# Loading sorted tokens in blocks of 128 slots, with a last block rounded up to sixteens, in place of equal blocks

## The chip, the cores and the metric

The kernel runs on one core of a Trainium2 chip. The core has a matrix engine (PE, whose weight loads are listed apart as PEld), a vector engine (DVE), a scalar engine (ACT), a general engine (POOL) and a queue engine that issues most transfers (SP). Transfers are carried by 16 DMA engines that all queues share. The metric is the device time of one execution in microseconds (us), given as the median of several runs.

## The reference

Three layers run one after the other on 4 sequences of 768 tokens: a gated linear attention, a mixture of eight experts in which each token goes to one expert, and a last layer whose product is normalised.

```
def _moe_ref(x, expert_emb, tau, w1, w2):              # x: 3072 x 384
    xn = x / (np.linalg.norm(x, axis=-1, keepdims=True) + 1e-06)
    en = expert_emb / (np.linalg.norm(expert_emb, axis=-1, keepdims=True) + 1e-06)
    logits = xn @ en.T / tau
    expert_idx = np.argmax(logits, axis=1)
    ...
    for e in range(E):                                  # 8 experts
        mask = expert_idx == e
        h = np.maximum(x[mask] @ w1[e], 0.0)            # 384 -> 1024
        out[mask] = gate_w[mask, None] * (h @ w2[e])    # 1024 -> 384

def reference(**kwargs):
    attn_out = _attn_ref(**attn_kwargs)                 # state = f * state + k v ; y = q state
    x = attn_out.transpose(0, 2, 1, 3).reshape(B * S, H * D)
    x = _moe_ref(x=x, **moe_kwargs)
    return _moe2_ref(x=x, **moe2_kwargs)                # x @ w_in, softmax times x, layer norm, @ w_out
```

## The kernel before

**Attention (lines 109 to 365).** Pairs of heads and chunks of 128 tokens are worked through in steps. At the end of a chunk the tokens' rows of 384 features (1.5 KB) stand in SBUF, and `route` gives each token a slot of its expert. An indirect transfer (L413) scatters the rows into `xs` in memory. Slot r of expert e is row 8r + e of `xs`, so the rows of one expert lie eight rows apart.

**Turns.** The experts are worked through in eight turns, ordered by falling numbers of tokens. The numbers of slots that a turn handles are fixed: `CAPS = (460, 432, 412, 404, 396, 392, 384, 378)`. I number the turns from 0, so turn 2 has 412 slots and turn 3 has 404. A turn has eight chunks of 128 hidden features. For each chunk g, `w_load` fetches a piece of the two weights (`w1s`, `w2s`, 192 KB each, two buffers each), `w_split` splits them into a high and a low part (ACT `w1h` L544, POOL `w1l` L545, ACT `w2h` L546, DVE `w2l` L547), `l1` makes nine products into `h` (L773), ACT and DVE make `hh` and `hl` from it (L777, L778), and `l2` adds nine products to `yacc` (L792), one chunk behind `l1`.

**The sorted tokens.** `x_load(e)` fetches a turn's rows of `xs` into `xin`, in equal blocks of slots: `NBLK` is 4 blocks for turns of more than 384 slots and 3 for the others. That makes 108 rows in a block for turn 1, 103 for turn 2, 101, 99, 98, then 128 for turn 6 and 126 for turn 7. One transfer brings all blocks of a turn; its partition dimension is the number of rows in a block. `x_T(e, kc)` transposes the blocks on PE into `xps` (L758), for each of the three pieces kc of 128 features, from where ACT and DVE split them into the turn's `xT` tiles (`x0h`/`x0l` for even turns, `x1h`/`x1l` for odd ones, L759, L760). `x_load(e + 2)` and the last `x_T(e + 1)` are emitted in the fifth chunk of turn e.

**Turn 0** goes another way: `x0_load` fetches its 460 slots in four transfers of 115 rows each (L475), before the last tokens are routed; `x0_in` adds them by products with the identity to `x0T` in PSUM (L488), and `x0_sel` adds the tokens of the last two chunks by products with indicators (L483).

**Order.** A scheduler that simulates the program in time fixes each engine's order of instructions when the kernel is built; on the chip each engine runs its list in order and stops at the first instruction whose inputs are not there. SP's list holds the loads of weights, tokens and of the next layer's weights (`d`, L855, decoded in between by DVE and POOL), so a transfer is issued only when everything ahead of it on SP has been issued.

```
def rows(buf, t):
    r = buf.rearrange("(r e) d -> e r d", e=E)[which(t), 0:CAPS[t], :]
    return r.rearrange("o (i p) d -> p (o i) d", i=NBLK[t])
```

Of the kernel before, what the change touches and what calls it, by code (L numbers as in the profile page):

```python
# [8 lines left out]
F32 = mybir.dt.float32  # L9
# [7 lines left out]
PSUM = bass.MemoryType.PSUM  # L17
DRAM = bass.MemoryType.DRAM

B, H, S, D = 4, 8, 768, 48  # L20
NP = H // 2            # head pairs
D2 = 2 * D             # features of a pair
DP = 64 + D            # their partitions: a head's features at 0, the other's at 64
GROUPS = (((0, 1), (1, 2), (2, 4)), ((0, 2), (2, 4)), ((0, 4),), ((0, 4),))   # head pairs of each batch, in turn
LEAD = 3
R = 6                  # consecutive tokens on a partition of the transposed loads
NPART = S // R         # 128
R2 = R // 2
CH = 128               # chunk of the linear attention
NCH = S // CH          # 6  # L30
E = 8
DM = H * D             # 384
F = 1024
NT = B * S             # 3072
CAP = 464              # slots of an expert on the fast path
# slots of the experts in the order of their turns: first the one that is ahead after FIRST tiles
# of tokens, then the others by falling numbers of tokens
CAPS = (460, 432, 412, 404, 396, 392, 384, 378)
FIRST = (B - 1) * NCH + 1
CT = 4  # L40
CTP = CAPS[0] // CT    # 115
NBLK = tuple(CT if n > 384 else 3 for n in CAPS)    # blocks of a turn's slots
NSLOT = E * CAP
KC = DM // 128         # 3
FC = F // 128          # 8
NTILE = B * NCH        # 24

# [35 lines left out]
def _build(ctx, tc, ins, outs):  # L83
    nc = tc.nc
    PE, DVE, ACT, POOL, SP = nc.tensor, nc.vector, nc.scalar, nc.gpsimd, nc.sync
# [13 lines left out]
    meta = dram.tile([NT, 2], F32, name="meta")     # a sorted token's number and gate  # L99
# [7 lines left out]
    ident = cst["ident"]  # L107

    # ------------------------------------------------------------------ attention
# [10 lines left out]
    loaded = {}  # L120
# [8 lines left out]
    # the pairs' features beside each other, with nothing between the heads' but zeros  # L129
# [9 lines left out]
    # persistent little tiles  # L139
# [21 lines left out]
    # the steps before the end at which the experts' first weights are loaded and split  # L161
# [3 lines left out]
    # stage A: per (batch, head pair), decays and scaled transposed q and k  # L165
# [70 lines left out]
    def stage_units():  # L236
        """the work that prepares the pairs, in the order of its emission"""
        last = B * NP
        u = [lambda: a_R(0), lambda: a_F(0), lambda: (a_G(0), a_K(0), a_Q(0), a_R(1))]
        for n in range(last):  # L240
            def hs0(n=n):
                if n + 1 < last:
                    a_F(n + 1)
            def hs1(n=n):
                if n > 0:
                    a_K(n)
                if n + 1 < last:
                    a_G(n + 1)
            def hs2(n=n):
                if n > 0:  # L250
                    a_Q(n)
                if n + 2 < last:
                    a_R(n + 2)
            u += [hs0, hs1, hs2]
        return u

    # stage B: steps (batch, head pairs, chunk)
# [113 lines left out]
    def route(b, c0, c1):  # L371
        """the chunks' tokens to slots of their experts: a list of small pieces of work"""
# [49 lines left out]
        # the gate  # L422
# [26 lines left out]
    def first():  # L449
        """the expert of the first turn: the one with the most tokens by now"""  # L450
        pc = psT.tile([128, E], F32, tag="t", name="counts0")
        PE.matmul(pc, lhsT=onesb, rhs=cum, start=True, stop=True)
        key, mx, num = (rp.tile([128, n], F32, tag="f" + t, name="f_" + t) for t, n in (("key", E), ("mx", 1), ("num", 1)))
        perm = rp.tile([1, 1], I32, tag="fperm", name="f_perm")
        DVE.scalar_tensor_tensor(key, pc, float(E), cst["small"][:, 0:E], ALU.mult, ALU.add)
        DVE.tensor_reduce(out=mx, in_=key, axis=AX.X, op=ALU.max)
        DVE.tensor_scalar(lead, key, mx[:, 0:1], None, ALU.is_equal)
        DVE.tensor_tensor(key, lead, cst["small"][:, E:], ALU.mult)
        DVE.tensor_reduce(out=num, in_=key, axis=AX.X, op=ALU.add)
        DVE.tensor_copy(perm, num[0:1])  # L460
        turn.extend(nc.values_load_multi_w_load_instructions(
            perm, engines=(mybir.EngineType.SP,), min_val=0, max_val=E - 1)[1])
        DVE.tensor_scalar(cst["row0"], cst["row0"], num[:, 0:1], None, ALU.add)

    # the first turn's tokens: those of the last chunks go to their columns by products with
    # their places' indicators, the others come from memory, and all meet in PSUM
    x0 = {}
    NEAR = 1               # of its blocks, those that go ahead of the last chunk's routing
    rank_after = [None]

    def x0_load():
        src = rows(xs, 0)
        x0["in"] = [tmp.tile([CTP, 2, DM], F32, tag="P", name=f"x0_{i}") for i in range(2)]
        for i in range(CT):
            SP.dma_start(x0["in"][i // 2][:, i % 2, :], src[:, i, :])  # L475
        x0["ps"] = [psA.tile([128, CAP], F32, tag="A", name=f"x0T_{kc}")[:, 0:CAPS[0]] for kc in range(KC - 1)]
        x0["ps"].append(psB.tile([128, CAP], F32, tag="kt", name="x0T_2")[:, 0:CAPS[0]])
        x0["n"] = 0
# [6 lines left out]
    def x0_in():  # L485
        def rows_in(i):
            for kc in range(KC):
                PE.matmul(x0["ps"][kc][:, i * CTP:(i + 1) * CTP], lhsT=x0["in"][i // 2][:, i % 2, kc * 128:kc * 128 + 128],  # L488
                          rhs=ident[:CTP, :CTP], start=False, stop=False)
        for kc in range(KC):  # L490
            x0_sel(NCH - 2, kc, False)
        for i in range(NEAR):
            rows_in(i)
        with tc.issue_after(rank_after[0]):
            for i in range(NEAR, CT):
                rows_in(i)
# [17 lines left out]
    # ------------------------------------------------------------------ experts' weights  # L514
# [4 lines left out]
    def which(t):  # L519
        """the expert of a turn"""  # L520
        return bass.ds(turn[t], 1)

    def rows(buf, t):
        """a turn's slots in memory"""
        r = buf.rearrange("(r e) d -> e r d", e=E)[which(t), 0:CAPS[t], :]
        return r.rearrange("o (i p) d -> p (o i) d", i=NBLK[t])

# [24 lines left out]
    # ---- program: prologue  # L552
# [41 lines left out]
    # normalised expert embeddings over tau into the projection matrix  # L594
# [18 lines left out]
    # how far the preparation of the pairs has to be at a step's end  # L613
# [67 lines left out]
    # ------------------------------------------------------------------ experts  # L681
    w2p = ctx.enter_context(tc.tile_pool(reuse_waits="tile", name="w2p", bufs=1, side="right"))
    xt2p = ctx.enter_context(tc.tile_pool(reuse_waits="tile", name="xt2", bufs=3, side="right"))
    # the experts' products, features by sorted tokens; what a turn writes past its own tokens the
    # next one covers
# [17 lines left out]
    def order():  # L703
        """the experts by falling numbers of tokens, after the first turn's"""
# [24 lines left out]
        # the sorted place of an expert's first token, by expert and by turn  # L729
# [13 lines left out]
    def x_load(e):  # L743
        n = NBLK[e]
        xin[e] = xinp.tile([128, CT, DM], F32, tag="xin", name=f"xin_{e}")[0:CAPS[e] // n, 0:n]
        SP.dma_start(xin[e], rows(xs, e))

    def x_T(e, kc):
        n, nb = CAPS[e], NBLK[e]
        bt = n // nb  # L750
        if kc == 0:
            xT[e] = xT[0] if e % 2 == 0 else xT1
        hi, lo = xT[e]
        if kc == 0:
            xps[e] = psX.tile([128, 2, 512], F32, tag="X", name=f"xps_{e}")
        ps = xps[e][:, kc % 2, 0:n]
        for i in range(nb):
            PE.transpose(ps[:, i * bt:(i + 1) * bt], xin[e][:, i, kc * 128:(kc + 1) * 128], ident[:bt, :bt])  # L758
        ACT.copy(hi[:, kc, 0:n], ps)  # L759
        DVE.tensor_tensor(lo[:, kc, 0:n], ps, hi[:, kc, 0:n].bitcast(F32), ALU.subtract)  # L760
# [22 lines left out]
    def l2(g):  # L783
        """the second product, features by slots"""
# [13 lines left out]
    # the sorted tokens' numbers and gates  # L798
    def rank_tokens():
        """the tokens' sorted places"""  # L800
# [34 lines left out]
    # second layer's weights: float64 words to float32, split in two parts  # L835
# [7 lines left out]
    def decode(u):  # L843
        """one part of a weight, in four steps that are emitted apart"""
# [32 lines left out]
    # every other tile's products stay in the one place, the others' in the other  # L877
# [18 lines left out]
    def m_sm(t, g):  # L896
        """g: the rows' gate, which scales all of a row's products alike"""
# [75 lines left out]
    # ------------------------------------------------------------------ last layer  # L973
# [197 lines left out]
    # is the fast path's answer good for these inputs?  # L1171
# [80 lines left out]
```

## Time and profile before

| | |
|---|---|
| three runs | 796.67, 800.58, 803.06 us, median 800.58 us |
| span of the profiled execution, first to last instruction | 776.1 us |
| time of the profiled execution outside its span | not listed for this execution; the median less the span is 24.5 us |
| PE busy | 676.3 us (87%) |
| DVE, ACT, POOL busy | 485.1, 377.0, 187.2 us |
| attention and routing | about the first 235 us of the span |
| the eight turns of the experts | about 235 to 535 us |
| last layer | the rest |

The span is what the trace covers. A line of waits says which engine stood still, for whom, how long in total, how often, and the longest. A row of the timeline gives the start, the duration, the engine and line, the operation, and in brackets the idle time just before it with what ended it. [...]

### The profile page before, as it was taken

To read this page: it belongs to the slowest core of one execution; us is meant where nothing else is said; L and a number is where in the kernel's file an instruction comes from. 1 tells how busy PE (TensorE), PEld (TensorE's weight loads), DVE (VectorE), ACT (ScalarE), POOL (GpSimd) and SP (SyncE) were. 2 spreads that over 40 slices of the span, in tenths; PEclk is the share of its full clock that TensorE was granted. 3 is DMA by queue.
4 is the path that set the end of the run, shared out by engine and by line. 5 is a ranking of instruction groups with operands and counts; after the bars stand their busy time and mean duration, and the time that the engine had idled before them with its cause. 6 is when DMAs were issued, how large, how long until landed. Compare 5 with 4: busy or idle time off the path is not lost.

```text
span 776.1 us, 12508 instructions
## 1 busy us (share of the span) xinstructions
PE 676.3 (87%) x4336; PEld 600.9 (77%) x4336; DVE 485.1 (63%) x1136; ACT 377.0 (49%) x913; POOL 187.2 (24%) x214
## 2 busy tenths in 40 slices
PE   4999999999887808509797999999999999999995
PEld 3766778778776608509697998999889999999994
DVE  3578778876757208507676776867576555666662
ACT  4668877764532205204343554553554445545452
POOL 4001031030516104406465333332011111111111
PEclk9999999999978768859997999999999999999998
DMA  9964436231432314214656565441000000000000
GB/s 193 359 199 126 122 113 160 62 93 21 144 93 80 105 61 122 71 51 109 140 106 148 127 176 158 141 138 52 0 22 21 21 22 21 21 30 23 21 22 35
DMA packets 91614, 72.29 MB, mean 93 GB/s; under 512 B 34788, under 2 KB 87334, under 8 KB 91542
## 3 DMA queue, kind: packets, MB, share of 16 engines
q1 hardware_dynamic: 87701, 61.94, 29.8%
q0 software_dynamic: 3840, 9.47, 3.4%
q8 instruction: 36, 0.59, 0.3%
q14 instruction: 37, 0.30, 0.2%
HBM read 56.23 MB, written 15.16 MB: 92 GB/s over the span
## 4 chain that ended last, share of the span: by engine, by line
issue 31%; PE 28%; DMA 19%; DVE 11%; ACT 4%; POOL 4%; SPq 1%; POOLq 0%; ACTq 0%; DVEq 0%
DMA w1s<-in_moe_w 15%; PE yacc L792 5%; PE h L773 5%; PE A L276 4%; POOL out L1020 3%; PE y L326 3%; PE px L349 2%; DVE w2l L547 2%; DVE G L211 2%; PE y L322 2%; DMA xin<-xs 2%; PE tf L173 1%; PE u L299 1%; PE tq L173 1%; DMA x<-xs 1%
## 5 line engine op out<-in xcount | busy, mean ns | idle before, releaser
L545 POOL TENSOR_TENSOR w1l<-w1s,w1h 128x384 fp32r<-128x384 f32 x64 | 67.1, 1049 | 168.1 <-ACT w1h L544 159.3
L547 DVE TENSOR_TENSOR w2l<-w2s,w2h 128x384 fp32r<-128x384 f32 x64 | 50.1, 783 | 70.3 <-ACT w2h L546 66.7
L544 ACT CAST w1h<-w1s 128x384 fp32r<-128x384 f32 x64 | 32.8, 513 | 118.9 <-DMA w1s<-in_moe_w 118.7
L792 PE MATMUL yacc<-hh,w2h 128*128 128x460 f32 (+7 forms) x192 | 72.6, 378 | 20.0 <-ACT hh L777 20.0
L1020 POOL DMA_INDIRECT out<-ot,rows x24 | 23.3, 973 | 211.0 <-ACT ot L1018 169.0
L792 PE MATMUL yacc<-hh,w2l 128*128 128x460 f32 (+7 forms) x192 | 70.4, 367 | 0.0
L1015 PE MATMUL o<-wout_h,lh 128*128 128x384 f32 x192 | 64.9, 338 | 0.3
L1015 PE MATMUL o<-wout_h,ll 128*128 128x384 f32 x192 | 64.9, 338 | 0.1
L1015 PE MATMUL o<-wout_l,lh 128*128 128x384 f32 x192 | 64.7, 337 | 0.0
L792 PE MATMUL yacc<-hl,w2h 128*128 128x460 f32 (+7 forms) x192 | 55.6, 365 | 6.9 <-DVE hl L778 6.9
L778 DVE SCALAR_TENSOR_TENSOR hl<-h,hh 128x460 fp32r<-128x460 f32 (+7 forms) x64 | 36.7, 574 | 38.3 <-ACT hh L777 38.1
L891 PE MATMUL h<-win_h,x2h 128*128 128x512 f32 x144 | 58.8, 408 | 0.7 <-DVE rr L905 0.7
L1006 DVE TENSOR_TENSOR ll<-lT,lh 128x512 fp32r<-128x512 f32 x48 | 31.2, 686 | 44.4 <-ACT lh L1005 44.4
L891 PE MATMUL h<-win_h,x2l 128*128 128x512 f32 x144 | 56.9, 395 | 0.0
L891 PE MATMUL h<-win_l,x2h 128*128 128x512 f32 x144 | 56.7, 394 | 0.0
L792 PEld LDWEIGHTS yacc<-hh,w2h 128*128 128x128 f32 x192 | 38.7, 202 | 21.4 <-ACT hh L777 20.3
L276 PE MATMUL A<-Q,K 48*128 48x128 f32 x384 | 52.2, 316 | 0.0
L777 ACT ACTIVATE hh<-h 128x460 fp32r<-128x460 f32 (+7 forms) x64 | 32.8, 512 | 37.0 <-PE h L773 26.2
L758 PE MATMUL xps<-c_ident,xin 108*128 108x108 f32 (+6 forms) x78 | 13.0, 287 | 40.9 <-DMA xin<-xs 39.9
L278 DVE TENSOR_TENSOR Am<-A,c_cmask 128x256 f32<-128x256 f32 (+2 forms) x84 | 35.8, 456 | 17.7 <-PE A L276 11.3
L276 PEld LDWEIGHTS A<-Q,K 48*128 48x128 f32 x384 | 38.0, 199 | 10.7 <-issue 5.1
L792 PEld LDWEIGHTS yacc<-hl,w2h 128*128 128x128 f32 x192 | 37.9, 201 | 9.0 <-DVE hl L778 8.0
(238 smaller groups left out, 1809.1 us busy)
## 6 DMA issues: line engine op xcount, KB each, us to landing
w1s<-in_moe_w SPq DMA_DIRECT2D x64, 192.0 KB, 3.5
w2s<-in_moe_w SPq DMA_DIRECT2D x64, 192.0 KB, 3.0
xs<-zt SPq DMA_DIRECT2D x14, 384.0 KB, 5.5
ldf<-in_f_logit SPq DMA_DIRECT2D x16, 288.0 KB, 3.1
ldk<-in_k SPq DMA_DIRECT2D x16, 288.0 KB, 3.4
ldq<-in_q SPq DMA_DIRECT2D x16, 288.0 KB, 4.4
v<-in_v SPq DMA_DIRECT2D x24, 192.0 KB, 2.7
d<-in_moe_w_in SPq DMA_DIRECT2D x6, 512.0 KB, 4.2
```

Source lines behind the costliest of these rows:

```text
L276: PE.matmul(pa[h][:, j], lhsT=Kc[j][rows_], rhs=Qc[rows_, j], start=True, stop=True)
L278: DVE.tensor_tensor(Am[:, h], pa[h], cst["cmask"].rearrange("p (o c) -> p o c", o=1).to_broadcast([CH, nj, CH]), ALU.mult)
L544: ACT.copy(ah, a)
L545: split_after[0] = POOL.tensor_tensor(al, a, ah.bitcast(F32), ALU.subtract).ins
L547: DVE.tensor_tensor(bl, b, bh.bitcast(F32), ALU.subtract)
L773: PE.matmul(ps, lhsT=wt[:, kc, :], rhs=xx[:, kc, 0:nt], start=(n == 0), stop=(n == 3 * KC - 1))
L777: ACT.activation(hh, ps, AF.Relu)
L778: dec_after[0] = DVE.scalar_tensor_tensor(hl, ps, 0.0, hh.bitcast(F32), ALU.max, ALU.subtract).ins
L792: PE.matmul(yacc[dc], lhsT=wt[:, dc * 128:(dc + 1) * 128], rhs=a, start=(fc == 0 and p == 0), stop=(fc == FC - 1 and p == 2))
L891: PE.matmul(hps[t][:, sl], lhsT=xx[:, kc, :], rhs=wt[:, kc, sl], start=(n == 0), stop=(n == 3 * KC - 1))
L1015: PE.matmul(ps, lhsT=a[:, fc, :], rhs=wt[:, fc, :], start=(n == 0), stop=(n == 3 * FC - 1))
L1020: ins_ = POOL.indirect_dma_start(out=out, out_offset=bass.IndirectOffsetOnAxis(ap=rows2[:, t, 0:1].bitcast(I32), axis=0), in_=ot, in_offse ...
```

## The change

Blocks of a turn's slots are now of 128 rows, and the last block holds what is left over: 76 slots in turn 0, 48, 28, 20, 12 and 8 in turns 1 to 5, a full block in turn 6 and 122 in turn 7. The new `rows_load` fetches all blocks of more than 112 slots by one transfer on 128 partitions. A smaller last block has a transfer of its own, with its number of rows rounded up to a multiple of 16 (80 rows in turn 0; 48, 32, 32, 16, 16 in turns 1 to 5). The transposes and the products with the identity take the same blocks, without the rounding. Turns 6 and 7 have no second transfer.

```
-CTP = CAPS[0] // CT    # 115
-NBLK = tuple(CT if n > 384 else 3 for n in CAPS)    # blocks of a turn's slots
...
     def x0_load():
-        src = rows(xs, 0)
-        x0["in"] = [tmp.tile([CTP, 2, DM], F32, tag="P", name=f"x0_{i}") for i in range(2)]
+        x0["in"] = [tmp.tile([128, 2, DM], F32, tag="P", name=f"x0_{i}") for i in range(2)]
         for i in range(CT):
-            SP.dma_start(x0["in"][i // 2][:, i % 2, :], src[:, i, :])
+            rows_load(x0["in"][i // 2][:, i % 2:i % 2 + 1, :], 0, i, i + 1)
...
         def rows_in(i):
+            bt = block(0, i)
             for kc in range(KC):
-                PE.matmul(x0["ps"][kc][:, i * CTP:(i + 1) * CTP], lhsT=x0["in"][i // 2][:, i % 2, kc * 128:kc * 128 + 128],
-                          rhs=ident[:CTP, :CTP], start=False, stop=False)
+                PE.matmul(x0["ps"][kc][:, i * 128:i * 128 + bt], lhsT=x0["in"][i // 2][:bt, i % 2, kc * 128:kc * 128 + 128],
+                          rhs=ident[:bt, :bt], start=False, stop=False)
...
-    def rows(buf, t):
-        """a turn's slots in memory"""
-        r = buf.rearrange("(r e) d -> e r d", e=E)[which(t), 0:CAPS[t], :]
-        return r.rearrange("o (i p) d -> p (o i) d", i=NBLK[t])
+    def block(t, i):
+        return min(128, CAPS[t] - i * 128)
+
+    def rows_load(dst, t, i0, i1):
+        src = xs.rearrange("(r e) d -> e r d", e=E)
+        full = [i for i in range(i0, i1) if block(t, i) > 112]
+        if full:
+            n = len(full)
+            r = src[which(t), i0 * 128:(i0 + n) * 128, :]
+            SP.dma_start(dst[:, 0:n, :], r.rearrange("o (i p) d -> p (o i) d", p=128))
+        for i in range(i0 + len(full), i1):
+            bt = -(-block(t, i) // 16) * 16
+            r = src[which(t), i * 128:i * 128 + bt, :]
+            SP.dma_start(dst[0:bt, i - i0, :], r.rearrange("o p d -> p (o d)"))
...
     def x_load(e):
-        n = NBLK[e]
-        xin[e] = xinp.tile([128, CT, DM], F32, tag="xin", name=f"xin_{e}")[0:CAPS[e] // n, 0:n]
-        SP.dma_start(xin[e], rows(xs, e))
+        xin[e] = xinp.tile([128, CT, DM], F32, tag="xin", name=f"xin_{e}")
+        rows_load(xin[e], e, 0, -(-CAPS[e] // 128))
...
-        for i in range(nb):
-            PE.transpose(ps[:, i * bt:(i + 1) * bt], xin[e][:, i, kc * 128:(kc + 1) * 128], ident[:bt, :bt])
+        for i in range(-(-n // 128)):
+            bt = block(e, i)
+            PE.transpose(ps[:, i * 128:i * 128 + bt], xin[e][:bt, i, kc * 128:(kc + 1) * 128], ident[:bt, :bt])
```

On SP, around the load of turn 2's tokens in turn 0, this stands before (an ISA row computes the address of the transfer behind it):

```order
L533 ISA
L533 DMA w2s_3541<-in_moe_w 128x384
L746 ISA
L746 DMA xin_3549<-xs 103x4x384
L531 ISA
L531 DMA w1s_3584<-in_moe_w 128x3x128
```

and this now:

```order
L544 ISA
L544 DMA w2s_3542<-in_moe_w 128x384
L533 ISA
L533 DMA xin_3550<-xs 128x3x384
L537 ISA
L537 DMA xin_3550<-xs 32x384
L542 ISA
L542 DMA w1s_3586<-in_moe_w 128x3x128
```

The load has become two, at the same place, and the next weights come behind both.

On SP, around the load of turn 3's tokens in turn 1, before (`d_3` is a part of the last layer's weights):

```order
L531 DMA w1s_3901<-in_moe_w 128x3x128
L855 DMA d_3_4118<-in_moe_w_in 128x512
L533 ISA
L533 DMA w2s_3903<-in_moe_w 128x384
L746 ISA
L746 DMA xin_3911<-xs 101x4x384
```

and now:

```order
L542 DMA w1s_3857<-in_moe_w 128x3x128
L865 DMA d_3_4121<-in_moe_w_in 128x512
L544 ISA
L544 DMA w2s_3859<-in_moe_w 128x384
L542 ISA
L542 DMA w1s_3903<-in_moe_w 128x3x128
L544 ISA
L544 DMA w2s_3905<-in_moe_w 128x384
L533 ISA
L533 DMA xin_3913<-xs 128x3x384
L537 ISA
L537 DMA xin_3913<-xs 32x384
```

Here `d_3` has moved ahead by one chunk's pair of weight loads as well.

On PE, where turn 3's first piece is transposed within turn 1, before:

```order
L773 MATMUL h_3953<-x1h,w1l_3892 128x432
L773 MATMUL h_3953<-x1l,w1h_3891 128x432
L758 MATMUL xps_4174<-c_ident,xin_3911 128x101 x4
L792 MATMUL yacc_0_3775<-hh_3923,w2h_3846 128x432
L792 MATMUL yacc_0_3775<-hh_3923,w2l_3847 128x432
L792 MATMUL yacc_1_3779<-hh_3923,w2h_3846 128x432
```

and now:

```order
L783 MATMUL h_3956<-x1h,w1l_3894 128x432
L783 MATMUL h_3956<-x1l,w1h_3893 128x432
L768 MATMUL xps_4177<-c_ident,xin_3913 128x128 x3
L768 MATMUL xps_4177<-c_ident,xin_3913 128x20
L802 MATMUL yacc_0_3777<-hh_3926,w2h_3848 128x432
L802 MATMUL yacc_0_3777<-hh_3926,w2l_3849 128x432
L802 MATMUL yacc_1_3781<-hh_3926,w2h_3848 128x432
```

The transposes stay at the same place, between the same products, four as before.

## Rows read from the trace of the kernel before

**Rows 1.** The page: its head, and PE's busy tenths in 40 slices of the span.

```profile
span 776.1 us, 12508 instructions
PE   4999999999887808509797999999999999999995
```

**Rows 2.** Waits of PE, 235 to 540 us: total, times, longest.

```profile
PE xps L758 <- DMA xin<-xs: 39.9, 6, 26.5
PE yacc L792 <- ACT hh L777: 20.0, 1, 20.0
PE yacc L792 <- DVE hl L778: 6.9, 3, 3.3
```

**Rows 3.** Timeline of PE: transposes and products behind a wait (start, duration, idle before).

```profile
258.88 0.98 PE L758 MATMUL xps<-c_ident,xin 108*128 108x108 f32 x4 [3.85 <-DMA xin<-xs]
293.41 0.75 PE L792 MATMUL yacc<-hh,w2h 128*128 128x460 f32 x1 [20.05 <-ACT hh L777]
348.02 0.91 PE L758 MATMUL xps<-c_ident,xin 101*128 101x101 f32 x4 [26.45 <-DMA xin<-xs]
385.61 0.86 PE L758 MATMUL xps<-c_ident,xin 99*128 99x99 f32 x4 [4.18 <-DMA xin<-xs]
420.69 0.89 PE L758 MATMUL xps<-c_ident,xin 98*128 98x98 f32 x4 [2.22 <-DMA xin<-xs]
452.25 0.52 PE L758 MATMUL xps<-c_ident,xin 128*128 128x128 f32 x3 [1.34 <-DMA xin<-xs]
481.07 0.73 PE L758 MATMUL xps<-c_ident,xin 126*128 126x126 f32 x3 [1.87 <-DMA xin<-xs]
```

**Rows 4.** Timeline of SP's queue: issues of turns 1 to 7's token loads, one weight load.

```profile
252.81 0.39 SPq L746 DMA_DIRECT2D xin<-xs  x1
262.21 0.26 SPq L746 DMA_DIRECT2D xin<-xs  x1
262.84 19.64 SPq L531 DMA_DIRECT2D w1s<-in_moe_w  x1
318.13 0.25 SPq L746 DMA_DIRECT2D xin<-xs  x1
378.31 0.32 SPq L746 DMA_DIRECT2D xin<-xs  x1
414.52 0.34 SPq L746 DMA_DIRECT2D xin<-xs  x1
447.30 0.38 SPq L746 DMA_DIRECT2D xin<-xs  x1
474.85 0.34 SPq L746 DMA_DIRECT2D xin<-xs  x1
```

**Rows 5.** DMA issues by size, the load for turn 2: KB.

```profile
xin<-xs SPq DMA_DIRECT2D x1, 618.0 KB
```

**Rows 6.** Windows: engines' busy time, then PEclk, DMA share, GB/s.

```profile
270.00:280.00 10.00, 3.36 (x19) 2.72 (x17) 0.00 (x0) 0.00 (x0) 0.00 (x0) 0.82 0.07 24
325.00:338.00 13.00, 0.00 (x0) 0.00 (x0) 0.00 (x0) 0.00 (x0) 0.00 (x0) 0.50 0.07 24
447.30:452.20 4.90, 3.61 (x20) 3.28 (x19) 2.53 (x4) 1.33 (x3) 1.02 (x1) 1.00 0.83 258
```

**Rows 7.** Timeline of ACT near the end of PE's wait in turn 0.

```profile
292.39 0.51 ACT L544 CAST w1h<-w1s 128x384 fp32r<-128x384 f32 x1 [24.52 <-DMA w1s<-in_moe_w]
```

**Rows 8.** Window just after that wait, columns as in Rows 6.

```profile
293.40:297.00 3.60, 3.59 (x10) 3.17 (x11) 3.60 (x7) 2.31 (x5) 1.72 (x2) 0.51 0.19 55
```

**Rows 9.** Turn 0's tokens: SP's four issues, PE's products with the identity.

```profile
224.53 1.71 SPq L475 DMA_DIRECT2D x<-xs  x4
228.06 1.12 PE L488 MATMUL x0T<-c_ident,x 115*128 115x115 f32 x6 [1.99 <-DMA x<-xs]
229.70 3.27 PE L488 MATMUL x0T<-c_ident,x 115*128 115x115 f32 x12 [0.51 <-DMA x<-xs]
233.66 1.63 PE L488 MATMUL x0T<-c_ident,x 115*128 115x115 f32 x6 [0.69 <-DMA x<-xs]
```

More of the change, by code (lines that the diff above doesn't have):

```diff
@@ L743, in x_load @@
     def x_load(e):
-        n = NBLK[e]
-        xin[e] = xinp.tile([128, CT, DM], F32, tag="xin", name=f"xin_{e}")[0:CAPS[e] // n, 0:n]
-        SP.dma_start(xin[e], rows(xs, e))
+        xin[e] = xinp.tile([128, CT, DM], F32, tag="xin", name=f"xin_{e}")
+        rows_load(xin[e], e, 0, -(-CAPS[e] // 128))
     def x_T(e, kc):
-        n, nb = CAPS[e], NBLK[e]
-        bt = n // nb
+        n = CAPS[e]
         if kc == 0:
```

## Prediction

> **What bounds the kernel now.** I read the page first. PE is busy nearly everywhere, except for two holes in the middle of the span, in the turns of the experts [rows 1]. The second view, the waits of PE in that stretch, names what ends them: 39.9 us for `xin`, the sorted tokens, and one wait of 20.0 us for `hh` [rows 2]. The timeline of PE shows how they are spread: the wait of 20.05 us ends at 293.41, one of 26.45 us ends at 348.02 in front of turn 3's transposes, and five waits of 1.34 to 4.18 us stand in front of the transposes of turns 1, 4, 5, 6 and 7 [rows 3].
>
> The third view, SP's queue, gives the age of each load when PE can start its transposes [rows 3, 4]: turn 1, 258.88 - 252.81 = 6.07 us; turn 3, 29.89; turn 4, 7.30; turn 5, 6.17; turn 6, 4.95; turn 7, 6.22. Turn 6's load is the only one on 128 partitions, and it is the fastest; turn 3's, of about the same size, takes six times as long. During the slow loads the DMA share is 0.07, about one engine of 16, and 24 GB/s move; during turn 6's load it is 0.83 and 258 GB/s [rows 6]. Turn 2's 618 KB [rows 5] are 632,832 bytes, which at 24 GB/s take 26.4 us. So the loads of 103 and 101 rows run on one DMA engine, and it is not memory or the eight-row stride that holds them, since turn 6's load has the same stride.
>
> The 20.05 us are the same thing seen from the side. Turn 2's load is issued at 262.21. The weights behind it need that engine too: SP itself is held 19.64 us on the next issue [rows 4], ACT waits 24.52 us for `w1s` until 292.39 [rows 7], and the `hh` that PE needs stands behind that cast in ACT's list. All engines are idle in these holes, so nothing useful is done in them that would come due later.
>
> [...]
>
> **The change part by part.** *Turn 3.* The load on 128 partitions takes turn 6's 4.95 us. The 32 rows of its last block come as a second transfer, issued one issue later, 0.63 us by the spacing at 262.21 to 262.84 [rows 4]. Its cost is between nothing (it lands with the first) and 49,152 bytes at the one-engine rate of 24 GB/s, 2.05 us (3.1 us for turn 1's 48 rows). I take 0.55 us, near the low end, since the four separate issues of turn 0's tokens follow each other in 1.71 us and land as a stream [rows 9]. So the age is 5.5 us: tokens at 318.13 + 5.5 = 323.6. PE arrives at 348.02 - 26.45 = 321.57 and waits 2.1 us. Gain 24.4.
>
> *Turn 2.* Its transposes are not late. With the load on 16 engines `w1s` behind it lands, at the slowest other age of 7.3 us, at 262.84 + 7.3 = 270.1; PE stopped at 293.41 - 20.05 = 273.36, and the cast and `hh` behind it take about 0.5 us each [rows 7]. So the whole 20.05 go. [...] Gain 21.8. [...]
>
> *Turns 1, 4, 5, 7.* Ages come down to 5.5 us (4.95 for turn 7, which has one transfer): 0.6 + 1.8 + 0.7 + 1.3 = 4.4. Turn 6 is unchanged.
>
> *Turn 0.* PE's three waits for the four loads of 115 rows are 1.99 + 0.51 + 0.69 = 3.2 us [rows 9]. The matmuls between them stay 24, with 460 columns in all, so the gain lies between 0 and 3.2; I take 2, since the first wait is mostly the time to a first landing.
>
> *Work that stays.* The transposes are as many as before, over the same number of columns, and stand at nearly the same places among PE's products. Five more issues cost SP 0.63 us each. SP waits for buffers most of the time, so it hides them, but right behind a token load they delay the next weights by that much; without the cover it would be 3.2 us in all.
>
> *What is late next.* In the stretches without a large hole PE waits for `hl` three times, 6.9 us in all [rows 2], when DVE, which also decodes the last layer's weights, falls behind. With the holes gone two turns' worth of such stretches is added, and the load of `d_3` stands one chunk earlier in SP's list, where it can hold the weights behind it until DVE has freed its buffer. I charge 2.6 us, about one more wait of the size of those three (0 to 7).
>
> The sum: 24.4 + 21.8 + 4.4 + 2.0 - 2.6 = 50.0 us off the span of 776.1 [rows 1], which gives 726. The median lies 24.5 us above that span; nothing outside the span is changed, so the time is 800.6 - 50 = **750.6 us**.
>
> [...]
>
> **The rivals.**
>
> [...]
>
> [...]
>
> *The loads stay slow: the other side.* If the rate were set by rows (1.5 KB pieces with a stride), not by the engines used, turns 2 and 3 would keep 26 us; then the change does not do what it says. The second loads would come on top: five issues of 0.63 us, and in turns 2 and 3 the last 32 rows at the slow rate, 2.05 us each, behind the others: 7 us, 808. It decides from an age of a 128-partition load of over 20 us. Against it stands turn 6's load with the same rows, stride and number of bytes at 4.95 us.
>
> **How the numbers follow.** The forecast has a chance of 0.72: 745 to 758 with the bounds of the small loads, turn 0 and the waits for `hl`. The weights' rival has 0.14 (757 to 766), more gain 0.10 (738 to 745), slow loads 0.03, and 0.01 is left for no change. From 740 to 762 some 0.85 of the chance is held, which leaves out the tails of two rivals. A difference of 1% (8 us) is about what a measurement of this kernel can tell. Faster by more than that: 0.96; within it 0.01; slower 0.03.
>
> **What would show it.** The DMA share during the two loads should be near 0.8, and SP's issue behind turn 2's load should take 0.4 us. PE's wait for `hh` should be gone, and its waits for `xin` should come to about 39.9 - 28.8 = 11 us, with about 2 us at turn 3. The forecast is wrong if waits for `hh`, `hl` or weights of over 8 us in total stand in the experts' stretch, if the second transfers land more than 2 us after the first, or if the hole at turn 3 is filled by another wait.

## The result, and the profile after

On one chip the changed kernel took 736.21 us (median of five, 724.77 to 738.45) against 800.58 (median of five, 789.51 to 804.8): a ratio of 0.9165, 95% interval 0.9048 to 0.9283 (the quotient of the medians is 0.9196). Two later comparisons, on two different chips, gave 0.9271 (0.9222 to 0.932) and 0.9303 (0.9242 to 0.9365). The three intervals share 0.9242 to 0.9283, so the first comparison probably lies low, and the change is worth about 7.4%, some 59 us of 800. The forecast was 750.6 us with a range from 740 to 762: the direction and the place were right, and the gain is larger than the 50 us that were worked out, by 9 us or, in the first comparison, by 14. As a share of 800.6 us the range begins at 0.924: the first comparison lies below that, the two later ones just inside.

The page of the kernel after: span, and PE's busy tenths in 40 slices. The two holes of [rows 1] are gone.

```profile
span 723.0 us, 12523 instructions
PE   4998998998988879999989999999999999999995
```

PE's waits from 225 to 520 us (total, times, longest), to be held against [rows 2]: 39.9 us for `xin` have become 10.8, where 11 were forecast, and 20.0 for `hh` have become 0.6. That the sum for `xin` agrees so well is in part luck: nothing of it stands at turn 3, where 2.1 was forecast, and turn 7's part is 1.75, where 0.6 was.

```profile
PE xps L768 <- DMA xin<-xs: 10.8, 5, 3.8
PE yacc L802 <- DVE hl L788: 1.6, 1, 1.6
PE xps L768 <- DVE x0l L770: 0.7, 1, 0.7
PE yacc L802 <- ACT hh L787: 0.6, 1, 0.6
```

SP's queue and PE's timeline answer to [rows 3, 4]. A load's issue, taken from the start of the transposes that waited for it, gives its age: 258.21 - 253.61 = 4.60 us for turn 1, 4.79 for turn 4, 5.03 for turn 5, 5.14 for turn 6. In two more profiles of the changed kernel (after_again, after_third) these are 4.39 and 4.24, 5.32 and 5.73, 5.32 and 6.47, 5.00 and 5.08.

```profile
253.61 0.40 SPq L533 DMA_DIRECT2D xin<-xs  x1
...
261.80 1.51 SPq L533 DMA_DIRECT2D xin<-xs  x1
263.51 0.34 SPq L537 DMA_DIRECT2D xin<-xs  x1
264.10 0.37 SPq L542 DMA_DIRECT2D w1s<-in_moe_w  x1
...
294.38 0.96 SPq L533 DMA_DIRECT2D xin<-xs  x1
...
328.41 0.38 SPq L533 DMA_DIRECT2D xin<-xs  x1
328.99 0.33 SPq L537 DMA_DIRECT2D xin<-xs  x1
...
362.56 0.38 SPq L533 DMA_DIRECT2D xin<-xs  x1
...
395.02 0.38 SPq L533 DMA_DIRECT2D xin<-xs  x1
```

```profile
258.21 0.74 PE L768 MATMUL xps<-c_ident,xin 128*128 128x128 f32 x4 [3.76 <-DMA xin<-xs]
301.38 0.71 PE L768 MATMUL xps<-c_ident,xin 128*128 128x128 f32 x4 [0.66 <-DVE x0l L770]
333.20 0.68 PE L768 MATMUL xps<-c_ident,xin 128*128 128x128 f32 x4 [1.66 <-DMA xin<-xs]
367.59 0.67 PE L768 MATMUL xps<-c_ident,xin 128*128 128x128 f32 x4 [1.98 <-DMA xin<-xs]
400.16 0.52 PE L768 MATMUL xps<-c_ident,xin 128*128 128x128 f32 x3 [1.64 <-DMA xin<-xs]
```

The weight load behind turn 2's tokens (264.10) holds SP for 0.37 us in place of 19.64; the issue of the tokens themselves (261.80) takes 1.51 in place of 0.26. In front of turn 3's transposes (301.38) PE no longer waits for tokens at all: they were asked for 7.0 us ahead (294.38). During the loads of turns 2 and 3 the DMA share, 0.07 before, is 0.71 and 0.70 (about 0.8 was forecast), and while turn 4's tokens land it is 1.04. The columns of the windows are those of [rows 6], where PEclk is PE's granted clock as a share of full speed; weights that land beside the tokens are in the GB/s.

```profile
261.80:267.00 5.20, 5.20 (x25) 4.45 (x25) 1.52 (x4) 2.21 (x5) 1.64 (x2) 0.93 0.71 226
294.40:299.00 4.60, 4.60 (x26) 4.18 (x25) 0.69 (x1) 0.20 (x1) 1.58 (x2) 1.00 0.70 140
330.50:333.00 2.50, 1.03 (x6) 0.68 (x4) 1.37 (x2) 0.18 (x1) 1.59 (x2) 1.00 1.04 350
```

From the issue of turn 1's load to turn 3's transposes the profiles give 348.02 - 252.81 = 95.2 us before and 301.38 - 253.61 = 47.8 after: 47.4 us less, where the forecast has 24.4 + 21.8 + 0.6 = 46.8. The repetitions give 96.1 before (same_again), 49.4 (after_again) and 46.3 (after_third) after.

### The profile page after: what moved, and what is told of

Same layout as the page of the kernel before. It is cut to its first block, busy times and chain, and to the rows that moved or that the text cites. A ratio compares the mean times of both kernels' runs of the same rounds, so it can differ in the third digit from the quotient of the medians.

```text
span 723.0 us, 12523 instructions
## 1 busy us (share of the span) xinstructions
PE 672.4 (93%) x4336; PEld 594.0 (82%) x4336; DVE 478.0 (66%) x1136; ACT 376.3 (52%) x913; POOL 187.3 (26%) x214
## 4 chain that ended last, share of the span: by engine, by line
issue 34%; PE 28%; DVE 13%; DMA 12%; ACT 6%; POOL 4%; SPq 2%; another core or an unknown queue 1%; POOLq 0%; ACTq 0%; DVEq 0%
DMA w1s<-in_moe_w 8%; PE A L274 5%; PE yacc L802 4%; PE h L783 4%; POOL out L1030 3%; DVE w2l L558 3%; PE y L324 3%; PE px L347 3%; PE y L320 2%; DVE G L209 2%; PE tf L171 2%; ACT w2h L557 1%; DMA xin<-xs 1%; PE tq L171 1%; PE u L297 1%
## 5 line engine op out<-in xcount | busy, mean ns | idle before, releaser
L802 PE MATMUL yacc<-hh,w2h 128*128 128x460 f32 (+7 forms) x192 | 70.6, 368 | 0.6 <-ACT hh L787 0.6
L802 PE MATMUL yacc<-hh,w2l 128*128 128x460 f32 (+7 forms) x192 | 68.5, 357 | 0.0
L787 ACT ACTIVATE hh<-h 128x460 fp32r<-128x460 f32 (+7 forms) x64 | 32.7, 512 | 24.9 <-PE h L783 15.2
L788 DVE SCALAR_TENSOR_TENSOR hl<-h,hh 128x460 fp32r<-128x460 f32 (+7 forms) x64 | 36.7, 573 | 13.2 <-ACT hh L787 13.1
L913 ACT ACTIVATE ex<-h,sm,rows 128x1024 f32<-128x1024 f32 x24 | 28.9, 1205 | 28.7 <-DVE sm L911 28.7
L904 DVE TENSOR_REDUCE sm<-h 128x1 f32<-128x512 f32 x48 | 33.0, 689 | 15.9 <-PE h L901 15.9
```

Of the source, the lines that this page charges most:

```text
L787: ACT.activation(hh, ps, AF.Relu)
L788: dec_after[0] = DVE.scalar_tensor_tensor(hl, ps, 0.0, hh.bitcast(F32), ALU.max, ALU.subtract).ins
L802: PE.matmul(yacc[dc], lhsT=wt[:, dc * 128:(dc + 1) * 128], rhs=a, start=(fc == 0 and p == 0), stop=(fc == FC - 1 and p == 2))
L904: DVE.tensor_reduce(out=sm[:, hf:hf + 1], in_=hps[t][:, sl], axis=AX.X, op=ALU.max)
```

## The experiments

Where a short diff says "turns", the turns named there load and transpose in the new blocks and all others in the equal blocks. Ratios are to the kernel before, run on the same chip beside them.

**The kernel before, once more (same_again).** No edit.

> The kernel before, unchanged. Open is where the 24.5 us between the median of 800.6 and the profiled span of 776.1 lie. Theory 1 (executions differ inside the span, little lies outside): spans and times of the same execution differ by about 2 us, as in the changed kernel (724.8 against 723.0), and the spans spread over 776 to 803. Theory 2 (some 24 us lie outside the span): times stay 24 us above their spans. Where executions differ, a profile of this one shows by stage which stretch differs: attention up to the load of turn 0 (224.5 us before), turn 0 to turn 1's load (28.3), to turn 3's transposes (95.2), the rest (428).

Measured: 787.1 us, ratio 0.9968 (0.9934 to 1.0003). The time is 1.7 to 1.9 us above the span in every execution of every kernel of this study. So the "24.5 us" of the prediction do not lie outside the span: executions differ inside it, and the one that was profiled was quick, for 776.1 + 1.8 is below all five times of the first comparison. By stage, the two profiles of the kernel before take 224.5 and 228.9 us up to turn 0's load, 28.3 and 23.2 from there to turn 1's load, 95.2 and 96.1 to turn 3's transposes, 428.1 and 429.0 for the rest.

**Only turns 2 and 3 (only_t23).**

```
-NEW = turns 0 to 7
+NEW = turns 2, 3
```

> New blocks for turns 2 and 3 alone, the other turns keep equal blocks. My theory (two loads on one engine make two holes of 20 and 26 us and the slow clock behind the first): faster by 46 us, ratio 0.942. Rival A (turn 0 and the loads of turns 1, 4, 5 and 7 bring as much as these two): faster by 30 us or less. Rival B (the weights take the hole's place behind the loads): waits of PE for hh of 4 us or more at turns 2 and 3. In the profile turn 1's load to turn 3's transposes takes 48 us in place of 95.

Measured: 741.09 against 789.56 us, 0.9369 (0.9298 to 0.944), 48.5 us. The two loads at about one engine's DMA share (0.07 [rows 6]) carry most of the gain, at the size forecast (46.2), which rules out rival A. From turn 1's load to turn 3's transposes it takes 49.0 us, where 48 were expected, and PE's only wait for `hh` is 0.9 us, which rules out rival B.

**Only turn 0 (only_x0, x0_again).**

```
+NEW = turn 0
```

> New blocks for turn 0's four loads alone. By the prediction: 2 us, ratio 0.997, within noise. By the profile after (28.3 us from these loads' issue to turn 1's load before, 19.1 after): 9 us, ratio 0.989. The two holes of PE at turns 2 and 3 stay (20 and 26 us).

> New blocks in turn 0 alone, a second time and with more executions. Prediction's term: -2 us, 0.9975. Earlier measurement: -9 us, 0.984 to 0.989, with the counts about 7 us behind the issue of the tokens in place of 13.

Measured: 0.984 (0.9792 to 0.9889), then with more executions 0.9895 (0.9848 to 0.9943); 9.2 and 8.0 us by the medians. The prediction's 2 us is too small, and so is its upper bound of 3.2.

**Only turns 1, 4, 5 and 7 (only_t1457, t1457_again).**

```
+NEW = turns 1, 4, 5, 7
```

> [...] By the prediction: 4.4 us, ratio 0.994. By the profile after, 6 us, ratio 0.992, nearly all of it at turn 4. [...] The two holes stay.

> New blocks in turns 1, 4, 5 and 7 alone, a second time and with more executions. If the prediction's term (the shorter ages, 4.4 us) is all of it: 0.9945 of before. If the earlier 8 to 10 us stand: 0.987 to 0.990, and then something beside the ages is in it, for the first profile showed PE's waits for tokens shorter by only 2.7 us.

Measured: 0.9868 (0.9806 to 0.9931) from four executions, then 0.996 (0.9936 to 0.9985) from twelve: 8.3 us first, 3.8 us then, and the two intervals do not meet. In the two profiles PE's waits for tokens come to 37.2 and 36.0 us against 39.9 before, shorter by 2.7 and 3.9, which agrees with the second number, as the forecast of 4.4 us does. That the first came of too few executions is likely and not shown; the second was also taken on another chip.

**106 rows, and 105 (rows106_t23, rows105_t23).** Turns 2 and 3 keep four equal blocks, of another length:

```
-        return CAPS[t] // 4                  # 103 and 101 rows
+        return 106 if t in (2, 3) else ...   # in the other kernel 105
```

> Turns 2 and 3 keep four equal blocks, but of 106 rows in place of 103 and 101; all else as before. [...] Theory 2 (equal blocks of about a hundred rows, or rows that do not fill 128 partitions, are slow as such): nothing changes, 0.995 to 1.005. Theory 3 (any row count that is not a prime is fast): -46 us, 0.94.

> As the run with 106 rows, but with 105, one row less in each block. [...] Theory 2: nothing changes, 0.995 to 1.005. [...]

Measured: 106 rows 0.9727 (0.9663 to 0.9792), 21.0 us, neither nothing nor 46; 105 rows 0.9402 (0.9342 to 0.9461), 48.6 us. One row less in each block is worth 27.6 us. With 106 rows both holes are there at about half length; these are SP's and PE's rows of that kernel, and between them a window while SP is held behind turn 2's tokens (columns as in [rows 6]). Its DMA share of 0.13, about two engines of 16, and its 48 GB/s are twice those of [rows 6]:

```profile
282.82 7.48 SPq L551 DMA_DIRECT2D w1s<-in_moe_w  x1
```

```profile
284.00:290.00 6.00, 6.00 (x32) 5.37 (x32) 1.75 (x4) 2.00 (x4) 1.02 (x1) 1.00 0.13 48
```

```profile
301.01 0.75 PE L811 MATMUL yacc<-hh,w2h 128*128 128x460 f32 x1 [7.86 <-ACT hh L796]
...
344.18 0.59 PE L777 MATMUL xps<-c_ident,xin 106*128 106x106 f32 x2 [14.23 <-DMA xin<-xs]
```

PE's wait in front of turn 3's transposes is 14.23 us with 106 rows, between 26.45 with 101 [rows 3] and 4.86 with 105. In that kernel of 105 rows the DMA share from 313 to 319 us, the last stretch ahead of those transposes, is 1.00, and 256 GB/s move:

```profile
313.00:319.00 6.00, 2.27 (x12) 1.84 (x10) 2.18 (x4) 0.81 (x2) 1.40 (x2) 1.00 1.00 256
```

```profile
320.12 0.59 PE L777 MATMUL xps<-c_ident,xin 105*128 105x105 f32 x2 [4.86 <-DMA xin<-xs]
```

If only the length of the blocks counted, 105 and 106 rows would give the same time. That equal blocks, or blocks under 128 rows, are slow as such is ruled out by 105 rows; that only primes are slow is ruled out by 106. So 101 and 103 rows go with a share of 0.07, 106 with 0.13 at turn 2 (0.32 at turn 3, from 330 to 340 us) and 105 with 1.00, the last two with all that lands beside the tokens; what in the number of rows sets the share, the runs don't show.

**Turn 0 with 120 rows (x0_120).** Three blocks of 120 slots and one of 100, loaded as 120 and 104 rows:

```
-        return CAPS[t] // 4                  # 115 rows in turn 0
+        return 120 if t == 0 else ...
```

> Turn 0 alone: three blocks of 120 slots and one of 100, loaded as 120, 120, 120 and 104 rows, in place of four of 115; all else as before. [...] Theory 2 (what counts are full blocks of 128 slots, for the products): 0 to -2 us, 0.997 to 1.0. The prediction's own term for turn 0 was -2 us.

Measured: 0.989 (0.9855 to 0.9925), 8.5 us, as with blocks of 128. In its profile PE goes through turn 0's products without a stop, at a granted clock of 1.00 from 246 to 251 us. It is the loads that count in turn 0, not full blocks.

**One transfer of 112 rows (equal112).** The changed kernel, with four blocks of 112 rows in turns 1 to 5 and no second transfer:

```
+        return 112 if t in (1, 2, 3, 4, 5) else 128
```

> The changed kernel, but turns 1 to 5 load four blocks of 112 rows (448 slots, 688 KB) in one transfer; there is no second small transfer. Theory 1 (the second transfers cost nothing on the path, as the trace of the changed kernel suggests): as the changed kernel, 0.912 to 0.921 of before, with ages of 5 to 6 us. Theory 2, the prediction's charge of 0.55 us each: 2.8 us less than the changed kernel. [...] Against a gain stands up to 22% more bytes in each load, some 0.5 us each at 258 GB/s.

Measured: 0.9331 (0.9251 to 0.9412), where 0.912 to 0.921 was expected if the second transfers cost nothing: no gain. It does not price the second transfers, since the loads themselves have become slower than those on 128 partitions: turn 4's was issued at 342.91 and ages 7.14 us, against 4.79, 5.32 and 5.73 for the pair of transfers in the three profiles of the changed kernel.

```profile
350.05 1.08 PE L777 MATMUL xps<-c_ident,xin 112*128 112x112 f32 x4 [4.03 <-DMA xin<-xs]
```

12% more bytes (672 KB against 576 and 24) do not explain a quarter to a half more time. The runs leave open what does.

**No rounding (no_round).** The last blocks with 76, 48, 28, 20, 12 and 8 rows.

```
-            bt = -(-block(t, i) // 16) * 16
+            bt = block(t, i)
```

> The changed kernel without the rounding: the last blocks are loaded with 76, 48, 28, 20, 12 and 8 rows. [...]

Measured: 0.9303 (0.9264 to 0.9342), beside 0.9271 (0.9222 to 0.932) for the changed kernel: not told apart, so the runs show no worth of the rounding. In turn 0 it takes 8.1 us from the issue of its tokens to the counts, against 7.2 with it.

**The changed kernel again, and two attempts at a better one (after_again, early, early_memset).** `early` asks for tokens one turn sooner:

```
+    x_load(2)
     for g in range(NG + 1):
...
-                if fc == 4 and e + 2 < E:
-                    x_load(e + 2)
+                if fc == 4 and e + 3 < E:
+                    x_load(e + 3)
```

and `early_memset` also moves the three clearings of `yT`:

```
-        if g < KC:
-                POOL.memset(yT[:, g, :], 0.0)
+        if 3 <= g < 3 + KC:
+                POOL.memset(yT[:, g - 3, :], 0.0)
```

> The changed kernel unchanged, so that the three runs beside it stand against it on the same chip: 0.905 to 0.928 of before. If the time of one execution differs inside the span (theory 1), time less span is 1.8 us in this run too, and the turn of the first token load comes at another time than 234.5 us, while from there to the end the spans agree within some 3 us.

> The changed kernel, with each turn's tokens asked for one turn earlier (three turns ahead in place of two; the buffer is free by then). [...] Rival 2 (the waits only move to the splits of DVE, the next thing late): no change.

> As the run with early token loads, and the three clearings of yT (9.0 us on POOL in one piece, ahead of the splits of the second chunk of turn 0) stand in the fourth to sixth chunk, one each. Theory 1 (DVE's cast of the experts' order, 3.2 to 6.3 us in nearly all profiles beside POOL's clearing and 0.31 us where the two do not meet, holds back turn 1's load): the cast takes 0.3 us, turn 1's load is issued 3 to 6 us earlier, and PE's wait of 3.8 us ahead of turn 1 goes: 3 to 5 us less than the run without it. Rival (POOL's clearing now holds back the splits of the weights' low part): no gain, or up to 3 us more.

Measured: 0.9271 (0.9222 to 0.932), 0.9253 (0.9205 to 0.93) and 0.9227 (0.9182 to 0.9272): no difference. `early` was to take away PE's four waits for tokens ahead of turns 4 to 7, 7.0 us in the profile after; its rival 2 came true. PE's waits from 300 to 545 us, first of the changed kernel, then of `early`:

```profile
PE xps L768 <- DMA xin<-xs: 7.3, 4, 2.3
PE xps L768 <- DVE x0l L770: 3.6, 3, 2.5
PE yacc L802 <- DVE hl L788: 1.9, 1, 1.9
```

```profile
PE xps L777 <- DVE x0l L779: 4.0, 4, 1.8
PE xps L777 <- DVE x1l L779: 3.1, 3, 1.8
PE yacc L811 <- DVE hl L797: 2.9, 4, 1.2
```

No wait for tokens is left there, and DVE holds PE for 10.0 us in place of 5.5. In these profiles DVE's splits are the next thing late once the tokens come in time, and the tokens' last 7 us are worth nothing alone. `early_memset` did not do its part: DVE's cast fell on a moved clearing and took 3.37 us, not the 0.3 expected, so its question stays open.

**The whole without turn 0, beside the whole (t1to7, after_third).**

```
+NEW = turns 1 to 7
```

> The whole change but turn 0. If turn 0 is worth 9 us with the holes gone as well: 9 us more than the changed kernel, 0.936 to 0.939 where that stands at 0.925 to 0.928. If its gain is taken back by a later wait once the holes are gone: the same as the changed kernel.

> The changed kernel, on the same chip as its parts. If the parts add up: its time falls by turns 2 and 3 (48.5 us) plus the two parts measured beside it. If they overlap: 3 to 8 us less than the sum. From the runs so far 0.917 to 0.927.

Measured on one chip: before 787.37 us, turns 1 to 7 alone 737.72 (0.9391, 0.9336 to 0.9445), the whole 732.01 (0.9303, 0.9242 to 0.9365). So turns 1 to 7 are worth 49.7 us by the medians and turn 0, added to them, 5.7, where 9 were expected; the two intervals of the ratios overlap slightly. The parts measured alone add up to 48.5 + 3.8 + 8.0 = 60.3 us, the whole gives 55.4 and not the 0.917 to 0.927 expected: the parts overlap by some 5 us, or it is scatter, which these intervals do not decide. The forecast for turns 1 to 7 is 24.4 + 21.8 + 4.4 - 2.6 = 48.0.

## Why the prediction fell short

**The term that was mis-sized: turn 0.** The prediction said: "The matmuls between them stay 24, with 460 columns in all, so the gain lies between 0 and 3.2; I take 2". It measured 8.0 to 9.2 us alone and 5.7 on top of the rest. The bound counted PE's waits only and left the products between the waits at their pace. But these ran at a granted clock of 0.50, behind PE's stops. Turn 0 of the run on turns 1 to 7, whose tokens come in 115 rows as before:

```profile
226.20 0.37 PE L481 MATMUL x0T<-sel,xlo 128*128 128x460 f32 x1
228.74 1.63 PE L487 MATMUL x0T<-c_ident,x 115*128 115x115 f32 x6 [2.17 <-DMA x<-xs]
...
230.31 3.29 PE L487 MATMUL x0T<-c_ident,x 115*128 115x115 f32 x12
234.46 1.63 PE L487 MATMUL x0T<-c_ident,x 115*128 115x115 f32 x6 [0.86 <-DMA x<-xs]
...
235.96 0.73 PE L481 MATMUL x0T<-sel,xhi 128*128 128x460 f32 x1
...
238.41 0.23 PE L734 MATMUL counts<-cum,onesb 128*128 128x8 bf16 x1
```

and the same place after the change:

```profile
235.51 0.37 PE L480 MATMUL x0T<-sel,xlo 128*128 128x460 f32 x1
237.00 0.94 PE L486 MATMUL x0T<-c_ident,x 128*128 128x128 f32 x6 [1.12 <-DMA x<-xs]
...
237.80 2.55 PE L486 MATMUL x0T<-c_ident,x 128*128 128x128 f32 x18
...
240.21 0.46 PE L480 MATMUL x0T<-sel,xhi 128*128 128x460 f32 x1
...
241.56 0.18 PE L725 MATMUL counts<-cum,onesb 128*128 128x8 bf16 x1
```

Twelve products in 3.29 us are 0.27 us each; eighteen in 2.55 us are 0.14. The six products with indicators behind them take 2.4 us (235.96 to 238.41) against 1.4. From the last product ahead of the tokens to the counts it is 12.2 us (226.20 to 238.41) against 6.1 (235.51 to 241.56). Of the 6.2 us between them the waits are 1.9 (2.17 + 0.86 against 1.12), the very 2 us that was forecast; the other 4.3 are the products, which the forecast held constant. The windows over the two stretches (columns as in [rows 6]) show a granted clock of 0.50 after stops of 2.17 and 0.86 us, and of 1.00 after one stop of 1.12. First the run on turns 1 to 7, then the changed kernel:

```profile
228.70:238.40 9.70, 8.77 (x32) 7.35 (x32) 1.52 (x6) 1.06 (x2) 1.93 (x2) 0.50 0.88 263
```

```profile
237.00:241.60 4.60, 4.53 (x34) 4.01 (x34) 0.99 (x6) 0.68 (x2) 1.21 (x2) 1.00 0.87 243
```

From SP's issue to the counts it takes 13.1 to 14.1 us in the eight profiles with 115 rows and 7.0 to 7.7 in the eight that load turn 0 as the changed kernel does: 6 to 7 us. Where the rest of the 8.0 to 9.2 measured alone lies, the runs don't show. This could have been read from [rows 9], where twelve products of 115 columns take 3.27 us; the granted clock there is 0.50 (229.50 to 238.00). For turn 2 the forecast has 1.75 us for the clock on top of the wait (21.8 against 20.05); for turn 0 it has none. The run with 120 rows shows that it is the row count of the load that decides: the counts come 8.3 us behind its issue, without full blocks. In the kernel before, with 115 rows, the DMA share is 0.32, about 5 engines of 16, and 114 GB/s move from 226 to 228 us, when these loads begin to land; in the changed kernel, the same time behind the issue, it is 0.90 with 290 GB/s (236 to 238).

**Turns 2 and 3: right.** 48.5 us alone against 46.2, and the rows behind them as forecast: SP freed after 0.37 us (0.4), no wait of weight for `hh`. The wait of 2.1 us that was left for turn 3 is there with these two turns alone, 1.60 us. In the whole it is not one for tokens, which are asked for 7.0 to 8.8 us ahead: PE is held there by DVE for 0.66, 2.46 and 1.13 us in the three profiles of the changed kernel. That the load is on 16 engines, as the forecast has it, no run shows; its DMA share is 0.71 (261.80 to 267.00), and from 258 to 300 us PE waits for turn 1's tokens alone (3.8 us). The 1.75 us for the clock, the part of the 21.8 beyond the 20.05 of the wait, are the author's estimate: 3.60 us at a granted clock of 0.51 [rows 8], counted as 3.60 x 0.51 at 1.00. No run shows this term by itself. In its place, the trace of the kernel before has nine products of 460 columns in 3.57 us behind the wait (293.41 to 296.98) and the next nine in 1.88 (296.98 to 298.86), 1.69 less; in the changed kernel the granted clock is 0.98 to 1.00 from 262 to 301 us.

**Turns 1, 4, 5 and 7: right**, 3.8 us against 4.4. The forecast age of 5.5 us is about what the pairs of transfers show: 4.24 to 4.60 at turn 1, 4.79 to 5.73 at turn 4, 5.03 to 6.47 at turn 5, against 5.00 to 5.14 for turn 6's single load. At turns 4 and 5 the pairs lie between 0.35 us ahead of the single load of the same profile and 1.39 behind it, so the charge of 0.55 us is neither shown nor ruled out.

**The charge of 2.6 us for `hl`.** It can't be separated. Waits for `hl` and `x0l`/`x1l` come to 7.8 us in the profile before and 3.9 in its repetition, and to 2.3, 8.7 and 7.6 in three profiles of the changed kernel. The sum for turns 1 to 7 is right with it.

**The base.** "The median lies 24.5 us above that span; nothing outside the span is changed" was wrong in its reading, without harm to the sum. The span itself varies, above all ahead of the change: SP's issue of turn 0's tokens, behind the same attention code, lies between 223.5 and 245.8 us in the profiles. It goes with the chip in the main: 238.8 to 243.8 where the kernel before took 801.05 us, 224.2 to 226.5 in three of four profiles where it took 787.37, and 237.2 in the fourth, a long execution of 789.83. The span that the prediction started from belongs to a quick execution (224.53); the times beside it were longer. From that issue to the end of the span the kernel before takes 551.6 and 548.3 us, the changed kernel 488.5, 495.0 and 495.8: 52 to 63 us less, and the profile shown above is the quickest of the three (after_again expected them within 3 us of each other).

**The rivals.** The weights' rival, in which the weights behind the loads of turns 2 and 3 come so late that they hold `hh` back again: PE waits 0.6 us for `hh`, ruled out. Loads that stay slow: ruled out by the ages. More gain (738 to 745) comes nearest, and turn 0 is one of its causes, by a larger step than the bound of 3.2 us. On the chip where parts and whole were measured together the gain is 55.4 us: of the 5.4 beyond the forecast turn 0 is 3.7, turns 1 to 7 are 1.7. The first comparison's 64 us lie 6 to 9 beyond what the two others show; no run explains that rest.

## What to carry to other kernels

Look at the number of rows in a transfer's blocks before anything else: one row more or less in a block moved this kernel by 27.6 us, and loads of 128 rows with a small rest aged 4.24 to 6.47 us, where even blocks of 98, 99, 108 and 112 rows aged 5.75 to 7.30 and one of 101 rows 29.89. Where a wait is removed, price the work that stands between and behind the waits at the clock it ran at and at the clock it will run at (0.50 and 1.00 in turn 0 here), also when the waits are as short as turn 0's 0.5 to 2.0 us. Compare executions of one chip, and repeat a part's effect of 1% before building on it.

## What the runs showed of the hardware

**In the attention PE does fewer instructions where the granted clock is lower.** Windows of the attention, whose code is the same, in the kernel before and in the run with 106 rows (columns as in [rows 6]): PE is busy for 88 to 97% of each, and does 182 and 176 instructions at 1.00, 133 at 0.74 and 104 at 0.66.

```profile
60.00:80.00 20.00, 19.41 (x182) 14.70 (x183) 16.59 (x38) 17.17 (x53) 1.88 (x5) 1.00 0.47 124
120.00:140.00 20.00, 19.23 (x176) 15.42 (x173) 17.35 (x37) 17.07 (x44) 2.39 (x6) 1.00 0.54 135
```

```profile
60.00:80.00 20.00, 18.99 (x133) 13.87 (x129) 13.91 (x29) 14.08 (x42) 1.39 (x4) 0.74 0.34 90
120.00:140.00 20.00, 17.63 (x104) 13.77 (x103) 11.55 (x19) 10.24 (x27) 3.04 (x6) 0.66 0.35 99
```

What lowers it there, the runs don't show.

**A small cast on DVE ends with one of POOL's clearings.** Three clearings of `yT` take 3.0 us each on POOL, one behind the other. DVE's cast of eight numbers in each partition starts during the first and ends within 0.1 us of the end of one of them. In the kernel before the clearings run from 240.01 to 249.04, and the cast ends with the third:

```profile
240.01 9.03 POOL L953 MEMSET yT<- 128x3536 f32 x3
242.78 6.29 DVE L726 CAST o_perm<-o_num 128x8 int32<-128x8 f32 x1
```

and in its repetition, where the clearings begin at 245.29, it starts 0.3 us ahead of the first one's end and ends with that:

```profile
245.29 9.08 POOL L953 MEMSET yT<- 128x3536 f32 x3
248.04 0.31 DVE L726 CAST o_perm<-o_num 128x8 int32<-128x8 f32 x1
```

Turn 1's load hangs on it: counts to issue take 15.2 us in the first case and 9.2 in the second. In the three profiles of the changed kernel the cast takes 3.23, 6.21 and 6.22 us, so it differs between executions of one kernel. What makes it wait, the runs don't show.

**SP is held longer behind a load with a lower DMA share.** In the kernel before, the next weights' issue behind the tokens of turns 2 and 3 takes 19.64 and 20.60 us, at a share of 0.07 [rows 6]. Behind turn 2's tokens with 106 rows it takes 7.48, at 0.13. In the changed kernel it takes 0.37 and 0.39, at 0.71 and 0.70.
